# Sliding-window attention feeding a mixture of experts: routing cut into short steps, the first expert slot in plain fp32, and two expert slots in a written-out order

## The chip, the cores and the metric

The kernel runs on one core of a Trainium2 chip. The number that counts is the device time of one execution in microseconds; lower is better. The chip's engines are called by the profile's short names: PE (TensorE, matmuls) with PEld (its weight loads), DVE (VectorE), ACT (ScalarE), POOL (GpSimd) and SP (SyncE, which here only issues transfers).

## The reference

Attention over 4 batches of 8 heads, 768 positions of 64 numbers, with a window of 128 positions and 4 sink positions that are always kept; its output is the input of a mixture of 8 experts, of which each of the 3072 tokens takes one:

```
keep = is_sink | in_window                    # 4 sinks, window 128
a = softmax(where(keep, q @ k.T / 8, -1e9))
x = (a @ v) as 3072 tokens x 512
e_idx = argmax(x @ w_gate)                    # one expert of 8 per token
gate_w = softmax(x @ w_gate)[e_idx]
eom = sigmoid(x @ w_output_gate)[e_idx]
out[token] = gate_w * eom * (relu(x @ w1[e_idx]) @ w2[e_idx])
```

An expert has w1 of 512 x 1024 and w2 of 1024 x 512, 4 MB together, so 8 transfers of 512 KB.

## The kernel before, in words

**Attention.** The 32 (batch, head) pairs are worked as 16 double heads, `NP = 16`. `pair_step(i)` is one step of a software pipeline: in three parts (g = 0, 1, 2) it makes the scores of double head i (PE, mask and maximum on DVE, exponential on ACT), and beside them the transpositions, sink rows, value products, normalisation and gate logits of double heads i-1 and i-2. Steps 16 to 18 have no scores and only drain the pipeline. The sink rows go through `sink`: ACT copies the high part, DVE subtracts the low part, and SP moves both into `psk` by DMA; `av_sink` needs them. In part 1 and 2 POOL scales the next double head's q (`scale`), and at the end of part 2 `gate2` of double head i-2 adds to the logits; with a batch's last double head it calls `batch_done`.

**Routing.** `gate_route` is a generator that works out, for the tokens of batches 0 and 1 together, then of batch 2, then of batch 3, which expert a token takes, its place in the expert's list (matmuls with a triangle of ones), its weight (`den`, written to DRAM beside x), and adds it to a table of token ids (`tab`) by a product of one-hot matrices (`ohrow`, `rhs`). After batch 1 and after batch 2, `rank_experts` orders the experts by their counts and `early_table` takes the rows of the two fullest ones: so expert slots 0 to 3 are fixed before all tokens are known. `final_table` makes the rest of the plan.

**The order of the work.** Everything in attention's loop stands under a manual schedule: PE, ACT, DVE and POOL do it in the order in which the program is written. SP's order, and that of everything behind the loop, is chosen by a scheduler that can also put later instructions between those of the loop. The routing's generators stand in a list `later`; `step()` runs the first one to its next `yield`, once per part g of an attention step (twice per part behind step 15). A list `behind` holds the conversions of weights, one per part.

**Expert slots.** A slot gathers up to 384 tokens by an indirect DMA from POOL (`gather`), turns them (`x_transpose`), and does two products (`mm1_group`, `mm2`). fp32 is split: a number is the sum of a high and a low fp32r part, and a product is three matmuls (high-high, high-low, low-high). So each 512 KB piece of weights goes through a staging buffer (`raw`, four of them), ACT rounds it to the high part and DVE or POOL subtracts to get the low one (`split` in `load_weights`, L454 and L455); the hidden layer is split in the same way (L489, L490), and x too (L484, L485). Slots with 64 tokens or fewer (`half1`, `half2`) use plain fp32 matmuls on the loaded weights (`whole`), with the array's columns in two halves. Weights live in rings of named buffers: a (4), b (3), c (6). Slots 0 and 1 have 256 tokens each.

## Time and profile before

| | us |
|---|---|
| median of 3 runs | 609.74 (605.77 to 613.70) |
| the profiled execution | 610.09 |
| its span | 607.8 |

Busy time in the span: PE 518.4 us (85%), DVE 357.1 (59%), POOL 328.7 (54%), ACT 283.2 (47%). The core moved 112.63 MB by DMA. The profile gives the span in 40 slices with the busy share of each engine in tenths; groups of instructions by line with their count, busy time and mean; the waits that ended last before an instruction (in brackets behind it, with the time its engine stood idle); and the chain of work that ended last. A matmul row's time is its latency; the distance between the starts of two of them is what they cost. Engines other than the one that sets the pace may stand idle at no cost, so shares are read stage by stage.

### The profile page before, as it was taken

How to read it: one execution, taken by the hardware profiler on the slowest of the kernel's cores; microseconds unless marked ns; L12 is line 12 of the kernel's file. 1: busy time of each engine (PE TensorE's matmuls, PEld its weight loads, DVE VectorE, ACT ScalarE, POOL GpSimd, SP SyncE). 2: the span in 40 equal slices, each digit the busy share in tenths (PEclk: the TensorE clock that was granted, in tenths of full speed). 3: DMA queues.
4: the chain of work that ended last, by engine and by line, in shares of the span. 5: the costliest groups of instructions: out<-in, count | busy, mean ns of one | idle time of the engine just before them, and what ended most of it. 6: DMA issues, size and time to landing. Idle time of an engine off the chain costs nothing.

```text
span 607.8 us, 10633 instructions
## 1 busy us (share of the span) xinstructions
PE 518.4 (85%) x3527; PEld 408.4 (67%) x3527; DVE 357.1 (59%) x762; ACT 283.2 (47%) x731; POOL 328.7 (54%) x345
## 2 busy tenths in 40 slices
PE   2999898978887625958899999989998989899992
PEld 1666665655555514947698897779876787777971
DVE  5577677777675589899936255324344736435520
ACT  3576666545444431443555244523352645446410
POOL 6466666746844462275566273573343777557510
PEclk9999999988898565978899999989997999999997
DMA  7378887775739264174685795562396785988660
GB/s 217 98 138 154 191 137 128 181 109 111 135 108 190 38 174 129 36 231 168 206 290 197 237 355 163 188 235 65 119 368 228 244 283 199 343 301 254 214 230 18
DMA packets 68673, 112.63 MB, mean 185 GB/s; under 512 B 8284, under 2 KB 34912, under 8 KB 68610
## 3 DMA queue, kind: packets, MB, share of 16 engines
q1 hardware_dynamic: 64146, 97.94, 56.8%
q0 software_dynamic: 4464, 13.91, 6.5%
q8 instruction: 31, 0.51, 0.4%
q14 instruction: 32, 0.26, 0.1%
HBM read 98.26 MB, written 13.25 MB: 183 GB/s over the span
## 4 chain that ended last, share of the span: by engine, by line
PE 43%; DVE 19%; DMA 15%; issue 9%; POOL 7%; ACT 5%; SPq 1%; POOLq 0%; ACTq 0%; DVEq 0%
PE s L510 16%; DMA raw<-in_w_dram 7%; PE oA L566 6%; PE oB L566 5%; PE s L672 5%; DMA out_dram<-y,idx 3%; PE oA L741 2%; ACT e L684 2%; PE tp L695 2%; DMA psk<-hl 2%; DVE s L678 1%; DVE nmx L682 1%; PE oB L741 1%; DMA xg<-xd,idx_e 1%; DMA xg<-xd,idx 1%
## 5 line engine op out<-in xcount | busy, mean ns | idle before, releaser
L684 ACT ACTIVATE e<-s,nmx 128x132 f32<-128x132 f32 x192 | 69.4, 366 | 76.1 <-DVE nmx L682 57.1
L672 PE MATMUL s<-kr,qr 64*128 64x260 f32 (+1 forms) x384 | 63.2, 438 | 19.1 <-ACT e L684 13.0
L81 POOL TENSOR_SCALAR_AFFINE_SELECT g<-f 128x512 f32<-128x512 f32 (+1 forms) x48 | 27.6, 575 | 72.1 <-ACT f L699 45.4
L490 DVE SCALAR_TENSOR_TENSOR hl<-s,hh 128x512 fp32r<-128x512 f32 (+1 forms) x40 | 29.6, 741 | 60.8 <-ACT hh L489 53.4
L672 PEld LDWEIGHTS s<-kr,qr 64*128 64x128 f32 x384 | 32.6, 203 | 39.8 <-ACT e L684 19.7
L552 POOL DMA_INDIRECT out_dram<-y,idx x20 | 25.2, 1260 | 48.0 <-DMA out_dram<-y,idx 11.7
L489 ACT ACTIVATE hh<-s 128x512 fp32r<-128x512 f32 (+1 forms) x40 | 25.5, 638 | 50.8 <-PE s L510 50.7
L682 DVE TENSOR_REDUCE nmx<-s 128x2 f32<-128x264 f32 x96 | 41.5, 433 | 3.3
L659 POOL TENSOR_SCALAR qr<-qr 128x256 f32<-128x256 f32 x48 | 41.1, 877 | 1.3 <-DMA qr<-in_qT_dram 1.2
L678 DVE COPY_PREDICATED s<-maskf,s 128x256 f32<-128x256 int32 x80 | 33.7, 421 | 11.8 <-PE s L672 8.8
L684 ACT ACTIVATION_READ_ACCUMULATOR e<-s,nmx 128x1 f32 x192 | 37.8, 197 | 0.0
L695 PE MATMUL tp<-ident,e 128*128 128x128 f32 x192 | 31.5, 307 | 5.5 <-ACT f L699 5.5
L695 PEld LDWEIGHTS tp<-ident,e 128*128 128x128 f32 x192 | 23.1, 154 | 17.5 <-ACT f L699 6.4
L81 POOL TENSOR_SCALAR_AFFINE_SELECT f<-f 128x512 f32<-128x512 f32 (+1 forms) x48 | 27.0, 562 | 3.3
L470 POOL DMA_INDIRECT xg<-xd,idx x21 | 24.3, 1158 | 7.2 <-issue 3.5
L741 PE MATMUL oA<-f,vt 128*64 128x128 f32 x256 | 28.0, 299 | 0.0
L455 POOL TENSOR_TENSOR a1l<-raw,a1h 128x1024 fp32r<-128x1024 f32 x5 | 12.3, 2467 | 17.9 <-PE oB L566 16.3
L482 PE MATMUL tp<-ident,xg 128*128 128x128 f32 x100 | 16.7, 298 | 6.1 <-DVE tab L274 3.3
L551 ACT ACTIVATE y<-oA,sc 128x512 f32<-128x512 f32 (+1 forms) x18 | 11.7, 650 | 21.3 <-PE oA L566 14.3
L455 POOL TENSOR_TENSOR a2l<-raw,a2h 128x1024 fp32r<-128x1024 f32 x5 | 14.4, 2880 | 10.1 <-ACT a2h L454 5.8
L741 PE MATMUL oA<-g,vt 128*64 128x128 f32 x192 | 19.5, 283 | 0.0
L741 PEld LDWEIGHTS oA<-f,vt 128*64 128x64 f32 x256 | 15.4, 144 | 6.1 <-issue 4.4
(560 smaller groups left out, 1711.8 us busy)
## 6 DMA issues: line engine op xcount, KB each, us to landing
raw<-in_w_dram SPq DMA_DIRECT2D x104, 512.0 KB
kr<-in_kx_dram SPq DMA_DIRECT2D x16, 396.0 KB
qr<-in_qT_dram SPq DMA_DIRECT2D x16, 384.0 KB
vt<-in_vx_dram SPq DMA_DIRECT2D x16, 384.0 KB
xd<-x SPq DMA_DIRECT2D x16, 384.0 KB
b1h<-in_w_dram SPq DMA_DIRECT2D x2, 512.0 KB
b1l<-in_w_dram SPq DMA_DIRECT2D x2, 512.0 KB
b2h<-in_w_dram SPq DMA_DIRECT2D x2, 512.0 KB
```

Source lines behind the costliest of these rows:

```text
L81: nc.gpsimd.affine_select(out=ap, in_=ap if src is None else src, pattern=pattern, compare_op=op, fill=fill, base=base, channel_multiplier=cm)
L455: b = eng.tensor_tensor(out=lo, in0=raw, in1=hi.bitcast(F32), op=ALU.subtract)
L490: nc.vector.scalar_tensor_tensor(out=lo, in0=ps, scalar=0.0, in1=hi.bitcast(F32), op0=ALU.max, op1=ALU.subtract)
L510: nc.tensor.matmul(out=ps[:, j, 0:n], lhsT=a, rhs=x[:, d, 0:n], start=d == 0 and i == 0, stop=d == ND - 1 and i == 2)
L566: nc.tensor.matmul(out=ys[s], lhsT=h[:, sl], rhs=x, start=f == 0 and i == 0, stop=f == NF - 1 and i == 2)
L659: nc.gpsimd.tensor_scalar(out=q, in0=q, scalar1=SCALE, scalar2=None, op0=ALU.mult)
L672: nc.tensor.matmul(out=s[:, a, o0:P + CW], lhsT=z["q"][r, t * P:(t + 1) * P], rhs=z["k"][r, k0:k0 + P + CW - o0], start=True, stop=True)
L678: nc.vector.copy_predicated(out=both[:, :, 4:CW], mask=bc(maski[:, 1, 4:CW], 1, 2), data=s[:, :, 0:P])
L682: nc.vector.tensor_reduce(out=m, in_=both, axis=AX.X, op=ALU.max, negate=True)
L684: nc.scalar.activation(out=z["e"][:, t, a, :], in_=both[:, a, :], func=AF.Exp, bias=m[:, a:a + 1], scale=1.0, accum_out=z["rs"][:, t, a:a ...
L695: nc.tensor.transpose(out=tp[:, k, :], in_=z["e"][:, 2 * j + k // 2, k % 2, 4:CW], identity=ident)
L741: nc.tensor.matmul(out=o, lhsT=v[:, kt, r], rhs=src[:, kt, a, :], start=t == kt == 0 or t == kt + 1 == 4, stop=False, skip_group_check=True)
```

## The change: what it does

- `gate_route`, `rank_experts`, `early_table` and `final_table` are cut into more and shorter steps, and every `yield` carries a letter. `point(name)` runs the first generator in `later` only if it waits at that letter. The loop has four such places per step: A in `sink` between ACT's high part and DVE's low part; B at the end of part 1; P behind the scores of part 2; C behind `av_sink`, ahead of `gate2`. Behind step 15 two further points per part take any letter.
- Of the three pieces of a one-hot product two go to POOL, issued together at A, and one to DVE at B, for every batch; before, all were POOL's, one per step (for the last batch DVE's).
- The experts are ranked as soon as the counts are known, ahead of the table; `taken` and `base` are updated there. Both expert numbers are read at that time, and 12 transfers of 512 KB are put in `behind`, one per part: slot 0's w1 and w2 straight into the a ring, without staging or split, and slot 1's w1 into the four staging buffers.
- Slot 0 is done in plain fp32 (`plain_x`, `plain1`, `plain2`) on 256 tokens.
- `early_slots` stands under the manual schedule: slots 0 and 1 in a fixed order, with routing steps (four behind each group of slot 0's matmuls, two in slot 1) and the conversions of slot 1's weights between them. The loop has one draining step fewer. `final_table` comes behind these slots; the scheduler may still move it.

```diff
-        def gate_route(bs, lg, e2=nc.vector):
+        def gate_route(bs, lg, counted=None):
...
-            yield
+            yield "A"
...
+            yield "B"
...
+            yield "C"
...
+            tt(out=eq, in0=og, in1=ohb, op=ALU.mult)
+            z = small([P, n], F32, "z")
+            nc.vector.tensor_reduce(out=z, in_=eq, axis=AX.X, op=ALU.add)
+            yield "P"
             nc.scalar.activation(out=dd, in_=dd, func=AF.Exp)
-            yield
+            nc.scalar.activation(out=z, in_=z, func=AF.Exp, scale=-1.0)
...
+            yield "C"
...
+            if counted is not None:
+                counted()
+            yield "A"
+            den = small([P, n], F32, "den")
+            nc.vector.tensor_reduce(out=den, in_=dd, axis=AX.X, op=ALU.add)
...
+                yield "A"
...
-                for t in range(0, T, 2):
-                    e2.tensor_tensor(out=rhs[:, t:t + 2], in0=bc(oh2[:, h + t:h + t + 2].rearrange("p t a e -> p t (a e)"), 3, NJ),
-                                     in1=bc(ohj[:, h + t:h + t + 2], 2, 2 * E), op=ALU.mult)
-                    if t < T - 2:
-                        yield
-                yield
+                for t, eng in ((0, nc.gpsimd), (2, nc.gpsimd), (4, nc.vector)):
+                    if t == 4:
+                        yield "B"
+                    eng.tensor_tensor(out=rhs[:, t:t + 2], in0=bc(oh2[:, h + t:h + t + 2].rearrange("p t a e -> p t (a e)"), 3, NJ),
+                                      in1=bc(ohj[:, h + t:h + t + 2], 2, 2 * E), op=ALU.mult)
+                yield "P"
...
@@ rank_experts, early_table
+            yield "C"
+            if r0:
+                nc.vector.tensor_copy(out=had, in_=taken)
+            for r in range(n):
+                tt(out=taken, in0=taken, in1=perm[:, r0 + r, :], op=ALU.add)
+            nc.vector.scalar_tensor_tensor(out=base, in0=taken, scalar=2.0 * P, in1=base, op0=ALU.mult, op1=ALU.max)
...
-                tt(out=four, in0=four, in1=bc(taken, 1, 4), op=ALU.mult)
+                tt(out=four, in0=four, in1=bc(had, 1, 4), op=ALU.mult)
...
@@ load_weights
+                    if parts:
+                        loads.append(lambda hi=hi, view=view: nc.sync.dma_start(out=hi, in_=view))
+                    else:
+                        nc.sync.dma_start(out=hi, in_=view)
...
+                raws = []
+                def load(view=view, raws=raws):
+                    raws.append(stg.tile([P, kk, n], F32, name="raw"))
+                    nc.sync.dma_start(out=raws[0], in_=view)
+                def cast(pool=pool, name=name):
+                    hi, lo = ((pool or pools[name[0]]).tile([P, kk, n], F32R, name=name + x) for x in "hl")
+                    his.extend(hi[:, j, :] for j in range(kk))
+                    los.extend(lo[:, j, :] for j in range(kk))
+                    return hi, lo
+                def split(raws=raws, cast=cast, eng=nc.vector if i % 2 else nc.gpsimd):
+                    hi, lo = cast()
+                    nc.scalar.copy(out=hi, in_=raws[0])
+                    eng.tensor_tensor(out=lo, in0=raws[0], in1=hi.bitcast(F32), op=ALU.subtract)
                 if parts:
+                    loads.append(load)
                     splits.append(split)
                 else:
+                    load()
                     split()
...
+        def plain1(mp, w, xf, f0):
+            ps = s_tile()
+            for j in range(2):
+                for d in range(ND):
+                    nc.tensor.matmul(out=ps[:, j, 0:2 * P], lhsT=w[0][d][:, (f0 + j) * P:(f0 + j + 1) * P], rhs=xf[:, d, 0:2 * P],
+                                     start=d == 0, stop=d == ND - 1)
+            h = mp.tile([P, 2, HN], F32R, name="hh", bufs=4).bitcast(F32)
+            nc.scalar.activation(out=h[:, :, 0:2 * P], in_=ps[:, :, 0:2 * P], func=AF.Relu)
+            return [h[:, 0], h[:, 1]]
+        def plain2(w, hs, ys, f):
+            for s, y in enumerate(ys):
+                nc.tensor.matmul(out=y, lhsT=hs[f][:, s * P:(s + 1) * P], rhs=w[0][f], start=f == 0, stop=f == NF - 1)
...
@@ ring, loop
+        aa, bb, cc = (["%s%d" % (c, i) for i in range(n)] for c, n in (("a", 4), ("b", 3), ("c", NB)))
+        order = iter(aa + bb + aa + bb[:1] + (cc + bb[1:] + aa + bb[:1]) * NSLOT)
...
                 nc.scalar.copy(out=hl[:, 0, :], in_=tp[0:n, 0, :])
+                point("A")
                 tt(out=hl[:, 1, :], in0=tp[0:n, 0, :], in1=hl[:, 0, :].bitcast(F32), op=ALU.subtract)
...
+            def start_later(g, at):
+                later.insert(at, [g, next(g)])
+            def point(name=None):
+                if later and name in (None, later[0][1]):
+                    x = later[0]
+                    x[1] = next(x[0], None)
+                    if x[1] is None:
+                        later.remove(x)
+                        r = [r for r, (after, n) in enumerate(ROUNDS) if after == b]
+                        start_later(gate_route(bs, bt["lg", bs], lambda: start_later(early_rank(r[0]), 0)) if r
+                                    else gate_route(bs, bt["lg", bs]), len(later))
+                        if r:
+                            start_later(early_rows(r[0]), len(later))
...
+            def early_rank(r):
+                yield from rank_experts(*firsts(r))
                 if r == 0:
-                    ws["e0"] = expert_reg(order_i[0:1, 0:1])
-                    ws[0, 0], rest = load_weights(0, ws["e0"], slot, parts=True)
-                    behind.append(split_later(rest, 4))
-                    yield
-                    yield
+                    for k in range(2):
+                        ws["e%d" % k] = expert_reg(order_i[0:1, k:k + 1])
+                    for j in range(2):
+                        ws[0, j], loads, _ = load_weights(j, ws["e0"], slot, whole=True, parts=True)
+                        behind.extend(loads)
+                    ws[1, 0], loads, splits[1, 0] = load_weights(0, ws["e1"], slot, parts=True)
+                    behind.extend(loads)
+            def early_rows(r):
+                yield from early_table(*firsts(r))
+                if r == 0:
                     ws["xg"] = early_gather(0)
...
+                    if g == 2 and i < NP:
+                        point("P")
...
+                        point("B")
...
+                        if i < NP:
+                            point("C")
                         if have(i - 2):
                             gate2(i - 2)
-                    for _ in range(1 if i < NP else 2):
-                        step()
-                    for x in behind:
-                        next(x, None)
+                    if i >= NP:
+                        if not behind and splits[1, 0][1:]:
+                            splits[1, 0].pop(0)()
+                        for _ in range(2):
+                            point()
+                    if behind:
+                        behind.pop(0)()
+            def early_slots():
...
+                for f in behind:
+                    f()
+                xf = plain_x(mx, ws["xg"])
+                while splits[1, 0][1:]:
+                    splits[1, 0].pop(0)()
+                h0 = []
+                for f0 in range(0, NF, 2):
+                    h0 += plain1(mp, ws[0, 0], xf, f0)
+                    between(4)
+                xg1 = early_gather(1)
+                begin(1, 1)
+                ys = [ps_o.tile([P, DM], F32, name=n) for n in ("oA", "oB")]
+                for f in range(NF):
+                    plain2(ws[0, 1], h0, ys, f)
+                    if f % 2:
+                        between(4, *([splits[1, 0].pop(0)] if f == 1 else [splits[1, 1].pop(0)] if f == 3 else []))
+                for s in range(2):
+                    put(mp, ys[s], ws["xg"][s][1], DM, out, NTOK, ids[0][s][1])
+                xs1 = x_transpose(mx, xg1)
+                h1 = []
+                for f0 in range(0, NF, 2):
+                    h1 += mm1_group(mp, ws[1, 0], xs1, 2, [f0])
+                    between(2, *([splits[1, 1].pop(0)] if f0 in (0, 2, 6) else []))
+                ys = [ps_o.tile([P, DM], F32, name=n) for n in ("oA", "oB")]
+                for f in range(0, NF, 2):
+                    mm2_part(ws[1, 1], h1, ys, (f, f + 1))
+                    between(2)
+                for s in range(2):
+                    put(mp, ys[s], xg1[s][1], DM, out, NTOK, ids[1][s][1])
...
-                for i in range(NP + 3):
-                    pair_step(i)
+                for i in range(NP + 2):
...
-            ws["xs"] = x_transpose(mx, ws["xg"])
-            while later:
-                step()
-            while len(hs0) < NF:
-                more0()
-            for x in behind:
-                for _ in x:
-                    pass
-            ws["e1"] = expert_reg(order_i[0:1, 1:2])
-            ws[1, 0] = load_weights(0, ws["e1"], slot, pin=True)
-            xgs1 = early_gather(1)
-            xs1 = x_transpose(mx, xgs1)
-            early = [[(idx_e[:, 0, r, j:j + 1], idx_e[:, 1, r, j:j + 1]) for j in range(2)] for r in range(NE)]
-            mm2(mp, ws[0, 1], hs0, ws["xg"], early[0])
-            hs1 = mm1(mp, ws[1, 0], xs1, 2)
+                    pair_step(i)
+                early_slots()
...
-            final_table(mp)
-            plan = [(order_i[0:1, r:r + 1], early[r], False) for r in range(NE)]
+            start_later(final_table(mp), len(later))
+            while later:
```

More of the change, by code (lines that the diff above doesn't have):

```diff
@@ L345, in early_table @@
                 nc.vector.tensor_reduce(out=idu[:, r, :], in_=pr, axis=AX.X, op=ALU.add)
-                tt(out=taken, in0=taken, in1=perm[:, r0 + r, :], op=ALU.add)
+            yield "C"
             ide = sm.tile([P, n, 2], F32, name="ide")
@@ L350, in early_table @@
             put_ids(idx_e[:, 0, r0:r0 + n], idx_e[:, 1, r0:r0 + n], ide)
[L351 removed]
         def final_table(mp):
             some = sm.tile([P, E, NJ], F32, name="some", bufs=1)
+            yield "A"
             tt(out=some, in0=bc(base, 2, NJ), in1=iouj, op=ALU.is_gt)
@@ L430, in moe_kernel, with load_weights @@
         w2v = w2.rearrange("e (f p) d -> e p f d", p=P)
-        def load_weights(which, ereg, slot, whole=False, parts=False, pin=False):
-            splits = []
+        def load_weights(which, ereg, slot, whole=False, parts=False):
+            loads, splits = [], []
             src, k, n = ((w1v, ND, FF), (w2v, NF, DM))[which]
@@ L515, in mm1_group, with plain_x, mm2_part @@
             return hs
+        def plain_x(mx, xgs):
+            xf = mx.tile([P, ND, HN], F32R, name="xh", bufs=1).bitcast(F32)
+            for s, (xg, sc) in enumerate(xgs):
+                nc.scalar.copy(out=sc, in_=xg[:, DM:XW])
+                tp = ps_t.tile([P, ND, P], F32, name="tp")
+                for d in range(ND):
+                    nc.tensor.transpose(out=tp[:, d, :], in_=xg[:, d * P:(d + 1) * P], identity=ident)
+                nc.scalar.copy(out=xf[:, :, s * P:(s + 1) * P], in_=tp)
+            return xf
+        def plain1(mp, w, xf, f0):
+            ps = s_tile()
+            for j in range(2):
+                for d in range(ND):
+                    nc.tensor.matmul(out=ps[:, j, 0:2 * P], lhsT=w[0][d][:, (f0 + j) * P:(f0 + j + 1) * P], rhs=xf[:, d, 0:2 * P],
[6 more added lines that the diff above has]
+                nc.tensor.matmul(out=y, lhsT=hs[f][:, s * P:(s + 1) * P], rhs=w[0][f], start=f == 0, stop=f == NF - 1)
+        def mm2_part(w, hs, ys, fs):
+            wh, wl = w
+            for f in fs:
+                hi, lo = hs[f]
+                for s, y in enumerate(ys):
+                    sl = slice(s * P, (s + 1) * P)
+                    for i, (h, x) in enumerate(((hi, wh[f]), (hi, wl[f]), (lo, wh[f]))):
+                        nc.tensor.matmul(out=y, lhsT=h[:, sl], rhs=x, start=f == 0 and i == 0, stop=f == NF - 1 and i == 2)
         def relu_transpose(mp, ps):
@@ L606, in moe_kernel @@
         ws = {}
-        ring = [["%s%d" % (c, i) for i in r] for c, r in (("a", range(2)), ("a", range(2, 4)), ("b", range(3)), ("c", range(NB)))]
-        a0, a1, b0, cc = ring
-        order = iter(a0 + a1 + b0 + a0 + a1 + b0 + a0 + (cc + a1 + b0 + a0) * NSLOT)
+        aa, bb, cc = (["%s%d" % (c, i) for i in range(n)] for c, n in (("a", 4), ("b", 3), ("c", NB)))
+        order = iter(aa + bb + aa + bb[:1] + (cc + bb[1:] + aa + bb[:1]) * NSLOT)
         pools = {"a": wp}
@@ L781, in moe_kernel @@
             later, behind = [], []
-            def split_later(fs, lag):
-                for _ in range(lag):
-                    yield
-                for f in fs:
-                    f()
-                    yield
-            def step():
-                if later and next(later[0], later) is later:
-                    later.pop(0)
+            def start_later(g, at):
[6 more added lines that the diff above has]
+                        later.remove(x)
             def batch_done(b):
@@ new lines, in pair_step, with between, begin @@
+                    if behind:
+                        behind.pop(0)()
+            def early_slots():
+                ids = [[(idx_e[:, 0, r, j:j + 1], idx_e[:, 1, r, j:j + 1]) for j in range(2)] for r in range(NE)]
+                ws["ids"] = ids
+                def between(n, *fs):
+                    for f in fs:
+                        f()
+                    for _ in range(n):
+                        point()
+                def begin(k, j):
+                    ws[k, j], loads, splits[k, j] = load_weights(j, ws["e%d" % k], slot, parts=True)
+                    for f in loads:
+                        f()
+                for f in behind:
+                    f()
+                xf = plain_x(mx, ws["xg"])
[25 more added lines that the diff above has]
+                    put(mp, ys[s], xg1[s][1], DM, out, NTOK, ids[1][s][1])
@@ L1074, in moe_kernel @@
             steps = []
-            for k in range(1, n):
-                if k > 1 and k not in ahead:
+            for k in range(2, n):
+                if k not in ahead:
                     steps.append((first, k))
```

67 lines of the change are left out of this document (24 added, 43 removed).

## The prediction

> **What bounds the kernel now.** I read the page's slices first, then a table of stages, then VectorE's timeline inside the attention loop, then the chain of waits for the prices.
>
> ```profile
> span 607.8 us, 10633 instructions
> PE   2999898978887625958899999989998989899992
> DVE  5577677777675589899936255324344736435520
> ```
>
> One slice is 15.2 us. Counted from 0, TensorE is nearly full up to slice 11, thin in 12 to 17 (7, 6, 2, 5, 9, 5), and full again from slice 20. VectorE has its 8s and 9s just there, in slices 14 to 19. The stage table (length, then busy time of PE, PEld, DVE, ACT, POOL, then clock, DMA share, GB/s) puts sizes on it:
>
> ```profile
> 72.00:104.00 32.00, 29.91 (x291) 20.10 (x291) 22.86 (x59) 20.02 (x88) 19.89 (x36) 1.00 0.79 145
> 114.75:200.50 85.75, 67.70 (x603) 46.33 (x599) 58.33 (x165) 42.22 (x185) 48.55 (x82) 0.91 0.64 130
> 200.50:238.70 38.20, 17.53 (x114) 12.24 (x114) 31.90 (x96) 12.03 (x22) 20.62 (x19) 0.59 0.48 113
> 238.70:304.90 66.20, 54.79 (x310) 48.18 (x311) 63.01 (x178) 27.49 (x38) 32.15 (x15) 0.87 0.50 165
> 304.90:600.00 295.10, 279.14 (x1612) 235.20 (x1610) 126.27 (x112) 132.19 (x193) 156.21 (x85) 0.98 0.66 232
> ```
>
> The rows are: the undisturbed attention loop; attention steps 10 to 15, where routing is mixed in (L, below); draining attention until the first expert matmul (D); expert slots 0 and 1 (S); the other slots. The first and the last are TensorE's. D and S are VectorE's: 31.90 of 38.20 us and 63.01 of 66.20. All that the change edits lies in L, D and S, 190 us together.
>
> Now L. These are VectorE's rows from step 9 into step 11; an L676 row opens a step.
>
> ```profile
> 104.09 0.49 DVE L676 COPY_PREDICATED_SCALAR s<-maskf,none 128x264 f32 x1 [0.15 <-PE s L672]
> 107.68 0.28 DVE L723 TENSOR_TENSOR hl<-oA,hl 40x128 fp32r<-40x128 f32 x1 [0.96 <-ACT hl L722]
> 111.24 0.43 DVE L678 COPY_PREDICATED s<-maskf,s 128x256 f32<-128x256 int32 x1 [0.61 <-PE s L672]
> 114.23 0.36 DVE L182 TENSOR_TENSOR lw<-tp,rs 128x192 f32<-128x192 f32 x1 [1.29 <-PE tp L180]
> 114.75 0.50 DVE L676 COPY_PREDICATED_SCALAR s<-maskf,none 128x264 f32 x1 [0.15 <-PE s L672]
> ...
> 118.55 0.23 DVE L208 TENSOR_REDUCE m<-lg 128x12 f32<-128x96 f32 x1
> 120.69 0.25 DVE L218 TENSOR_TENSOR dd<-lg,m 128x96 f32<-128x96 f32 x1
> ...
> 123.53 0.19 DVE L228 TENSOR_REDUCE den<-dd 128x12 f32<-128x96 f32 x1
> 124.37 0.17 DVE L236 TENSOR_TENSOR base<-tp,base 128x8 f32<-128x8 f32 x1
> ...
> 129.19 0.28 DVE L238 TENSOR_TENSOR pos<-pos,ohb 128x96 f32<-128x96 f32 x1
> 130.33 0.23 DVE L243 RECIPROCAL den<-den 128x12 f32<-128x12 f32 x1 [0.21 <-DVE den L242]
> 130.48 0.46 DVE L676 COPY_PREDICATED_SCALAR s<-maskf,none 128x264 f32 x1
> ```
>
> Step 9 takes 114.75 - 104.09 = 10.66 us and holds three idle times of VectorE: 0.96, 0.61 and 1.29. Step 10 takes 15.73, 5.07 more. Its routing comes in three lumps, 118.55 to 120.94, 123.53 to 124.54 and 129.19 to 130.56: 2.39 + 1.01 + 1.37 = 4.77. So nearly all of a lump is paid in full: it stands ahead of the next score's mask, and TensorE waits for that.
>
> **L, the loop.** The new points are just those idles: A in front of the 0.96, B at the 0.61, C in front of the 1.29, P without VectorE work. At 10.66 a step, steps 10 to 15 would take 64.0. To that I add what does not fit:
> - The first lump's six pieces take 0.40 each, the second's five 0.20. In step 10 A has two (0.8 of 0.96), B two (0.2 over the 0.61), C two of either kind (1.2 of 1.29). Ranking, positions and weights are cut in like pieces: I allow 0.4 over in each of steps 11 to 13, and 0.8 once for the position matmuls and two exponentials now at P. Sum 2.2.
> - Steps 14 and 15 hold the one-hot products, priced by these rows:
>
> ```profile
> L265 POOL TENSOR_TENSOR rhs<-oh,ohj 128x512 bf16<-128x512 bf16 x9 | 11.0, 1226 | 2.0 <-DVE oh L258 2.0
> L265 DVE TENSOR_TENSOR rhs<-oh,ohj 128x512 bf16<-128x512 bf16 x3 | 6.4, 2152 | 0.0
> 139.22 0.90 DVE L262 TENSOR_TENSOR ohrow<-io,jf 128x768 bf16<-128x768 f32 x1
> 215.52 3.09 DVE L262 TENSOR_TENSOR ohrow<-io,jf 128x768 bf16<-128x768 f32 x1
> ```
>
> The third product goes to VectorE at B: 2.15 - 0.61 = 1.5 over; for the table's six matmuls at P I allow 0.5. Two steps: 4.0. The 0.90 for ohrow just fits A; if GpSimd blocks it as in the 3.09 row, 2.2 more per step. GpSimd's two products, 2.45 us, delay the scaling of q; I count 0.5. [...]
> - DMA. Twelve loads of 512 KB (first slot whole, half of the second) are now issued one per third of a step from step 12, 6.3 MB in some 50 us, 126 GB/s. Free room behind the last q and k loads:
>
> ```profile
> 160.00:180.00 20.00, 17.35 (x156) 11.69 (x151) 13.67 (x40) 9.06 (x40) 13.74 (x22) 0.91 0.26 72
> 65.65 4.63 DMA psk<-hl
> ```
>
> Share 0.26 after step 13; before it 0.79 with 145 GB/s, which leaves less than the loads ask for one step. SyncE's queue is passed by them, and the sink rows' transfer (psk, 4.63 us) sits behind them. Between 0 and one landing per step (4.09, below), that is 0 to 16; I take 2, since only step 13 is oversubscribed.
>
> L after: 64.0 + 2.2 + 4.0 + 0.5 + 2 = 73, from 85.75: **13 saved** (0 to 20).
>
> **D, the drain.** One thing here leaves for certain: ScalarE's copy for the first slot's gather stood in front of attention's exponentials.
>
> ```profile
> 198.70 0.19 ACT L479 COPY sc<-xg 128x1 f32<-128x1 f32 x1 [4.07 <-DMA xg<-xd,idx_e]
> 200.93 1.33 PE L695 MATMUL tp<-ident,e 128*128 128x128 f32 x5 [5.50 <-ACT f L699]
> 224.01 0.15 DVE L298 SCALAR_TENSOR_TENSOR u<-taken,base 128x8 f32<-128x8 f32 x1
> 228.76 0.16 DVE L351 SCALAR_TENSOR_TENSOR base<-taken,base 128x8 f32<-128x8 f32 x1
> 230.82 0.19 DVE L208 TENSOR_REDUCE m<-lg 128x6 f32<-128x48 f32 x1
> 234.28 0.13 DVE L249 CAST pi<-tokpos 128x6 int32<-128x6 f32 x1
> ```
>
> (That 5.5 lies at the end of L; the copy is now behind the drain. It makes L's number safer, and I don't count it twice.) In D itself the order is now fixed: two short passes of attention, up to 15 points, and three of the second slot's conversions. VectorE's work there: the first rows of the table about 2.6; batch 2's routing to its positions 3.5 (230.82 to 234.28) and about 1.2 behind; ranking 2.0 (part of the 4.9 from 224.01); attention's own pieces about 5 (by the rows of step 9); one conversion 1.2 to 3.2: some 16 us. Beside it runs attention's own chain through psk's 4.63; two passes without scores should not be longer than two steps of L, 21. I take 19 for D (14 to 26), against 38.20: **19 saved**. The conversions of slot 0 and the routing of batch 3, which filled D, are gone or behind.
>
> **S, the two slots.** Prices of TensorE, from the chain of waits:
>
> ```profile
> 238.69 7.40 PE s L510 x46
> 250.04 2.82 PE s L510 x24
> 303.64 0.70 PE oA L566 x3
> 469.11 3.58 PE s L585 x16
> 377.45 4.09 DMA raw<-in_w_dram
> L485 DVE TENSOR_TENSOR xl<-tp,xh 128x512 fp32r<-128x512 f32 x25 | 16.5, 681 | 4.8 <-ACT xh L484 4.8
> L490 DVE SCALAR_TENSOR_TENSOR hl<-s,hh 128x512 fp32r<-128x512 f32 (+1 forms) x40 | 29.6, 741 | 60.8 <-ACT hh L489 53.4 <-issue 7.2
> L455 DVE TENSOR_TENSOR a1l<-raw,a1h 128x1024 fp32r<-128x1024 f32 x4 | 12.6, 3161 | 4.0 <-issue 4.0
> ```
>
> A slot in three split products costs 4 x 2.82 + 16 x 0.70 = 22.5; two make 45.0, so S loses 21 us to VectorE today. Plain fp32: L585 does eight half-width matmuls of 512 columns (16 records) in 3.58, two halves of the array side by side if they overlap. A full one then takes 3.58 / 4 = 0.90, or 0.45 if they don't. Slot 0 has 16 + 16 of that size: 28.6, or 14.3. I take 28.6, as the rows nearest in kind share the array by halves. So fp32 costs 6.1 more on TensorE. It takes off VectorE four conversions (up to 3.16 each), two 0.68 and four 0.74: 9 to 17 us, in the engine that bounds S. S after: 28.6 + 22.5 + a cold start 2.0 (46 matmuls in 7.40, at 2.82 / 24 they are 5.4) + 3 for turning the second slot's rows between the slots (four dependent pieces like the 0.68) + 4 for waits at the 20 routing steps left = **60, 6 saved** (-8 to 20). The final table's work on VectorE moves behind S; slots 2 and 3 hide it, whose rows don't need it (without that cover it would lengthen the stage by its own time, as in S before).
>
> The other slots keep their code. Four staging buffers serve slot 1 until its first product is over, so slot 2's last load may come late: 0 to 4.09 + 3.16; I take 2.
>
> **Sum:** 13 + 19 + 6 - 2 = 36 off the profiled run's 610.09 us (span 607.8): 574. The runs' median, 609.74, is 0.35 less: **574 us**, 5.9% less. A measurement of this kernel can tell about 2% from no change, so below 597.5 is faster and above 622 slower.
>
> **Rivals.** (1) The loop keeps its length: the loads collide with psk, or GpSimd blocks VectorE's steps (3.09 against 0.90). For it: share 0.79. Against it: share 0.26 from step 13. L's 13 are lost: 587. (2) The fixed order makes TensorE wait at the routing steps between the matmuls, as S lost 21 us before; S is then 28.6 + 22.5 + 21 + 5 = 77, so 17 worse: 591. Against it: plain fp32 needs no VectorE between its matmuls. (3) Slower: those same waits keep the clock at half. It was 0.59 in D, and the cold start shows its price. If the 51 us of matmuls in S run at half, they take 51 more: 625. It decides from 36 us at half on. Against it: the 24 matmuls at 250.04 already ran at the speed of later slots. [...] (4) Both (1) and (2): 604, no measurable change. (5) The change does better: the split halves of L585 don't overlap, 14.3 off: 560.
>
> **Chances:** forecast 0.57 (own range 562 to 583), (1) 0.13, (2) 0.12, (3) 0.03, (4) 0.08, (5) 0.07. Faster 0.89, same 0.08, slower 0.03. Range 550 to 594: it holds the forecast, (1), (2) and (5), and goes below (5) for L's and D's upper bounds together.
>
> **What will show it.** L: steps 10 to 13 at 10.7 to 11.5 us, 14 and 15 below 13.5; no VectorE routing row over 1 us at A or C; psk not among TensorE's waits. D: the first expert matmul 17 to 22 us behind the last exponential, no ACT wait for xg among exponentials. S: plain fp32 matmuls of 512 columns 0.90 us apart and VectorE well under 63 busy us. It is wrong if steps 10 to 15 stay over 80 us, if S stays over 66, or if slot 2 starts more than 5 us behind slot 1's end.

## The result, and the profile after

586.5 us (median of four runs, 583.9 to 588.8) against 609.4 us before (four runs). The ratio is 0.962, with an interval of 0.954 to 0.970. The profiled run took 584.36 us, its span was 582.1 us, 25.7 less than the 607.8 before. So the kernel is faster, and the time lies in the range, but some 12 us above the forecast of 574. The stages show that the total hides two misses and a gain that nobody forecast.

The first view is the table by stage of the kernel after: attention steps 10 to 15 (L), the drain up to the first expert product (D), slots 0 and 1 (S), and the other slots up to the last scaled output. The columns are the stretch, its length, the busy time of PE, PEld, DVE, ACT and POOL, the granted clock, the DMA share and GB/s.

```profile
114.16:198.28 84.12, 62.83 (x591) 42.65 (x589) 56.36 (x154) 41.50 (x182) 45.03 (x77) 0.88 0.77 172
198.28:219.42 21.14, 12.22 (x114) 8.28 (x110) 16.37 (x61) 8.22 (x18) 11.84 (x14) 0.79 0.63 133
219.42:287.94 68.52, 59.26 (x276) 44.01 (x276) 59.83 (x215) 22.67 (x36) 29.83 (x20) 0.94 0.39 122
287.94:571.90 283.96, 273.73 (x1613) 231.03 (x1611) 115.91 (x112) 133.24 (x194) 154.68 (x85) 1.00 0.69 242
```

Of the kernel before, the other slots up to the same end, and its first two rows of expert products:

```profile
304.87:597.61 292.74, 279.17 (x1612) 235.22 (x1610) 126.30 (x112) 132.19 (x193) 155.23 (x84) 0.98 0.67 233
235.29 0.80 PE L510 MATMUL s<-xh,a0h 128*128 128x256 f32 x2 [0.76 <-ACT xh L484]
238.69 0.58 PE L510 MATMUL s<-xl,a0h 128*128 128x256 f32 x1 [2.61 <-DVE xl L485]
```

Against the rows of before: L is 1.6 us shorter (forecast 13), D 17.1 (19), S 2.3 longer (forecast 6 shorter). The other slots, from 304.87 to 597.61 us before, were 292.7 us and are 284.0, 8.7 less (forecast 2 more). With the 0.6 that step 10 starts earlier these are the 25.7. One boundary matters: the prediction's D ends at 238.7 us, but the kernel before made a first pair of expert products at 235.29 and then waited 2.61 us. Measured to the first product, as after, D is 13.7 us shorter and S 1.1 shorter; their sum is the same.

L is not slow everywhere. By the first masks of the steps, steps 10 to 15 last 10.3, 10.7, 11.1, 29.6, 12.2 and some 10 us. What is lost lies in step 13. The next rows are of that step: TensorE's wait, VectorE's end of the sink rows, and SyncE's issues (start, time).

```profile
173.65 0.66 PE L815 MATMUL oA<-psk,vst 64*128 64x384 f32 x1 [17.68 <-DMA psk<-hl]
150.12 0.28 DVE L790 TENSOR_TENSOR hl<-oA,hl 40x128 fp32r<-40x128 f32 x1
145.52 0.37 SPq L469 DMA_DIRECT2D a0h<-in_w_dram  x1
...
153.62 0.37 SPq L469 DMA_DIRECT2D a3l<-in_w_dram  x1
154.61 0.47 SPq L479 DMA_DIRECT2D raw<-in_w_dram  x1
155.95 3.43 SPq L250 DMA_DIRECT2D xd<-den  x2
159.49 4.15 SPq L792 DMA_DIRECT2D psk<-hl  x3
```

The sink rows were ready at 150.4. SyncE issued them from 159.5, behind nine weight loads (eight tiles of slot 0 and one of slot 1, 4.7 MB, all between 145.5 and 155.1) and behind two writes of the gates' factors (den). They landed only some ten us after that. The written order puts one load behind each third of a step, but that order binds TensorE, ScalarE, VectorE and GpSimd, not SyncE: in the program's data the loads depended on nothing but the expert's number, and the scheduler put them together. The stretch in slices of 5 us shows two kinds of full DMA engines:

```profile
150.00:155.00 5.00, 5.00 (x56) 3.74 (x54) 4.58 (x15) 2.02 (x10) 4.27 (x6) 1.00 1.05 375
155.00:160.00 5.00, 0.97 (x18) 0.73 (x14) 1.20 (x5) 1.91 (x9) 0.81 (x2) 0.96 1.04 395
165.00:170.00 5.00, 0.00 (x0) 0.00 (x0) 0.00 (x0) 0.00 (x0) 0.00 (x0) 0.50 1.18 84
```

First weights at 375 to 395 GB/s, later a share of 1.18 at 84 GB/s. In S the rows to read are plain fp32's pace and the one long wait inside slot 0:

```profile
254.06 1.02 PE L573 MATMUL oB<-a3l,hh 128*128 128x512 f32 x2
254.91 0.59 PE L573 MATMUL oA<-a3l,hh 128*128 128x512 f32 x1
239.52 3.37 DVE L490 TENSOR_TENSOR a0l<-raw,a0h 128x1024 fp32r<-128x1024 f32 x1
242.82 0.95 DVE L268 TENSOR_TENSOR ohrow<-io,jf 128x768 bf16<-128x768 f32 x1
243.82 0.28 PE L278 MATMUL tp<-rhs,ohrow 128*128 128x256 bf16 x1 [3.52 <-DVE ohrow L268]
246.00:248.00 2.00, 2.00 (x4) 0.88 (x3) 2.00 (x13) 0.12 (x1) 0.00 (x0) 0.50 0.62 251
273.83 0.39 PE L542 MATMUL s<-xh,b0h 128*128 128x256 f32 x1 [2.91 <-DVE hl L522]
```

Two records make one product of 512 columns, 0.85 us apart (0.86 over several). One conversion of slot 1's weights stands ahead of the one-hot rows on VectorE, and TensorE waits 3.5 us for them; the clock is at half behind that.

### The profile page after: what moved, and what is told of

Same layout as the page of the kernel before. It is cut to its first block, busy times and chain, and to the rows that moved or that the text cites. A ratio compares the mean times of both kernels' runs of the same rounds, so it can differ in the third digit from the quotient of the medians.

```text
span 582.1 us, 10501 instructions
## 1 busy us (share of the span) xinstructions
PE 507.0 (87%) x3479; PEld 392.2 (67%) x3479; DVE 326.1 (56%) x754; ACT 274.8 (47%) x723; POOL 313.5 (54%) x340
## 5 line engine op out<-in xcount | busy, mean ns | idle before, releaser
L738 PE MATMUL s<-kr,qr 64*128 64x260 f32 (+1 forms) x384 | 61.9, 430 | 13.2 <-ACT e L750 6.6
L522 DVE SCALAR_TENSOR_TENSOR hl<-s,hh 128x512 fp32r<-128x512 f32 (+1 forms) x36 | 26.7, 747 | 58.7 <-ACT hh L521 49.6
L738 PEld LDWEIGHTS s<-kr,qr 64*128 64x128 f32 x384 | 31.9, 201 | 34.6 <-ACT e L750 15.6
L619 POOL DMA_INDIRECT out_dram<-y,idx x20 | 23.4, 1170 | 48.4 <-DMA out_dram<-y,idx 8.5
L521 ACT ACTIVATE hh<-s 128x512 fp32r<-128x512 f32 (+1 forms) x36 | 22.9, 642 | 30.4 <-PE s L542 30.4
L761 PE MATMUL tp<-ident,e 128*128 128x128 f32 x192 | 30.2, 296 | 0.0
L761 PEld LDWEIGHTS tp<-ident,e 128*128 128x128 f32 x192 | 22.2, 149 | 10.7 <-issue 5.4
L808 PE MATMUL oA<-f,vt 128*64 128x128 f32 x256 | 26.4, 285 | 0.0
L182 DVE TENSOR_TENSOR lw<-tp,rs 128x192 f32<-128x192 f32 x16 | 5.7, 354 | 34.3 <-PE tp L180 34.3
L815 PE MATMUL oA<-psk,vst 64*128 64x384 f32 x16 | 7.2, 450 | 19.3 <-DMA psk<-hl 19.2
L618 ACT ACTIVATE y<-oA,sc 128x512 f32<-128x512 f32 (+1 forms) x18 | 11.7, 650 | 22.1 <-PE oA L633 14.3
L818 ACT COPY ot<-oA 128x512 f32<-128x512 f32 x16 | 9.6, 599 | 22.8 <-PE oA L815 19.3
L765 ACT COPY f<-tp 128x512 f32<-128x512 f32 x32 | 18.6, 582 | 0.7 <-PE tp L761 0.7
```

Of the source, the lines that this page charges most:

```text
L521: nc.scalar.activation(out=hi, in_=ps, func=AF.Relu)
L522: nc.vector.scalar_tensor_tensor(out=lo, in0=ps, scalar=0.0, in1=hi.bitcast(F32), op0=ALU.max, op1=ALU.subtract)
L619: nc.gpsimd.indirect_dma_start(out=where, out_offset=bass.IndirectOffsetOnAxis(ap=ids, axis=0), in_=y, in_offset=None, bounds_check=rows - ...
L738: nc.tensor.matmul(out=s[:, a, o0:P + CW], lhsT=z["q"][r, t * P:(t + 1) * P], rhs=z["k"][r, k0:k0 + P + CW - o0], start=True, stop=True)
L761: nc.tensor.transpose(out=tp[:, k, :], in_=z["e"][:, 2 * j + k // 2, k % 2, 4:CW], identity=ident)
L808: nc.tensor.matmul(out=o, lhsT=v[:, kt, r], rhs=src[:, kt, a, :], start=t == kt == 0 or t == kt + 1 == 4, stop=False, skip_group_check=True)
```

## Experiments

Twelve kernels. Step lengths and stretches are of their profiled runs. L runs from step 10's first mask to the last exponential, D from there to the first expert product, S from there to slot 2's first product; "rest" from there to the last scaled output.

**1. Paced loads.** GpSimd touches each weight tile ahead of its load, so that the written order binds the load too.

```
+    nc.gpsimd.memset(hi[:, 0, 0:1], 0.0)
     nc.sync.dma_start(out=hi, in_=view)
...
+    nc.gpsimd.memset(raws[0][:, 0, 0:1], 0.0)
     nc.sync.dma_start(out=raws[0], in_=view)
```

> Edit: a one-element write by GpSimd into each of the twelve weight tiles goes ahead of its load, so that the load cannot start before GpSimd's written order reaches that third of a step. Theory (nine of the twelve loads left SyncE in one burst at the start of step 13, and step 13's three psk copies stood behind them): psk's wait falls from 17.7 us to 2 us or less, step 13 lasts 11 to 13 us instead of 29.6, steps 10 to 15 last 66 to 70 us in all, and the time is 567 to 573 us. Rival (6.3 MB of weights do not fit beside the loop's own transfers at any pace): psk's wait is spread over steps 13 to 15, steps 10 to 15 last 78 us or more, and the time is 579 to 586 us.

Measured: 580.8 us, ratio 0.959 (0.953 to 0.965). L is 70.7 us instead of 84.0, step 13 is 15.8, and its wait is 4.1. SyncE's issues of step 13 and the wait (paced kernel):

```profile
148.92 0.35 SPq L471 DMA_DIRECT2D a0h<-in_w_dram  x1
150.20 0.77 SPq L797 DMA_DIRECT2D psk<-hl  x1
151.08 1.00 SPq L250 DMA_DIRECT2D xd<-den  x2
152.13 1.67 SPq L797 DMA_DIRECT2D psk<-hl  x2
160.36 0.41 PE L820 MATMUL oA<-psk,vst 64*128 64x384 f32 x1 [4.12 <-DMA psk<-hl]
113.79:184.58 70.79, 61.52 (x591) 42.02 (x589) 56.32 (x154) 41.62 (x182) 45.32 (x86) 0.98 0.88 168
```

So the burst cost L 13 us, and for the loop the theory holds but for the last 2 us of wait. For the whole it failed: the profiled span is only 4.2 us shorter, and the ratio is not clear of the changed kernel's 0.962. D took back 2.8 (24.0), S 1.4 (69.95), the rest 3.1, and the last output's end 2.2. What remains of psk's wait is not the burst.

**2. All loads behind the loop** (on experiment 1).

```
+    for _ in range(4 if i >= NP else 0):
         if behind:
             behind.pop(0)()
```

> Edit: as the paced one, and all twelve loads come after the last score, four behind each third of the first drain step. Theory of the burst: steps 10 to 15 last 64 to 67 us, no psk wait above 1 us; 6.3 MB at the 375 to 395 GB/s of the burst take 16 to 17 us and end inside the drain's 20 us, so the time is 565 to 570 us. Rival (the loads then stand in front of the last rows' writes and the first gather): the drain grows from 19.9 us to 25 us or more, and the time is 572 to 580 us.

Measured: 594.9 us, ratio 0.979 (0.974 to 0.984). The rival, and worse than it said: the first load left at 197.9 us, 9.3 behind the last exponential, and D was 36.5 us. The surprise is in the loop. With no weight moving, step 13 was 17.6 us:

```profile
155.00:160.00 5.00, 3.44 (x42) 2.46 (x38) 3.33 (x13) 2.58 (x13) 2.29 (x5) 1.00 0.85 78
160.00:165.00 5.00, 0.88 (x3) 0.58 (x4) 0.00 (x0) 0.19 (x1) 0.32 (x1) 0.70 1.00 100
164.12 0.66 PE L820 MATMUL oA<-psk,vst 64*128 64x384 f32 x1 [5.68 <-DMA psk<-hl]
```

The DMA engines are nearly full (share 0.85 and 1.00) at 78 to 100 GB/s. What had been issued there beyond every step's own transfers were den's two writes, 768 packets of 4 bytes each. That these packets made the wait is an estimate from these rows; how they would fill the engines the rows do not show. Experiments 5, 6 and 9 move them.

**3. Routing's points at the ends of the thirds** (on experiment 1).

```
-    point("A") ... point("P") ... point("B") ... point("C")
+    else:
+        for _ in range(2 if g == 2 else 1):
+            point()
```

> Edit: as the paced one, and the same short steps of routing are taken at the ends of a step's three thirds (one, one and two), as the kernel before took its long ones, instead of at the four points inside. Theory of the prediction (each piece is paid where it stands ahead of the next score's mask): steps 10 to 15 are 10 to 18 us longer than in the paced kernel, some 80 us, and the time is 579 to 588 us. Rival (short pieces and the three products on GpSimd are what helps, the place is not): steps 10 to 15 within 4 us of the paced kernel's, and the time within 5 us of it.

Measured: four runs from 590.7 to 603.5 us. The profiled run took 601.4 us; its L is 84.6 us, 13.9 above experiment 1. The clock was full until 114 us and 0.75 to 0.91 in several stretches behind that; whether that came of the waits in the loop or of the run is not known, so the 13.9 are no price. The shortest run points the same way: 590.7 is 5.7 above the slowest and 11.1 above the fastest of experiment 1 (579.6 to 585.0). It is a single run, so the places' worth is shown in its direction, not in its size.

**4. Routing ahead of the conversion in slot 0** (on experiment 1).

```
-    between(4, *([splits[1, 0].pop(0)] if f == 1 else ...))
+    if f == 1:
+        between(4)
+    between(0 if f == 1 else 4, *([splits[1, 0].pop(0)] if f == 1 else ...))
```

> Edit: as the paced one, and in slot 0's second product the four steps of routing come ahead of the 3.4 us conversion of slot 1's weights on VectorE instead of behind it. Theory (that conversion holds the one-hot rows back, TensorE waits 3.5 us for them and then runs at half clock for some 5 us): the wait falls below 1.5 us, slots 0 and 1 last 3 to 6 us less than in the paced kernel, and so does the whole. Rival (TensorE waits for something else next: the table's pieces, or the converted weights at slot 1's start): the stretch stays within 1.5 us of the paced kernel's.

Measured: 584.0 us, ratio 0.961 (0.954 to 0.969). The 3.5 us wait went, and slot 0 ended 4.9 us sooner behind its first product (31.5 against 36.4 to the first scaled output). A new wait stood at slot 1's rows, and S came to 71.0 us:

```profile
246.40 1.04 ACT L494 CAST c1h<-raw 128x1024 fp32r<-128x1024 f32 x1 [3.76 <-DMA raw<-in_w_dram]
248.79 0.47 PE L519 MATMUL tp<-ident,xg 128*128 128x128 f32 x1 [6.80 <-DVE xl L522]
```

The rival. c1h is a tile of slot 2: its conversion is bound by no written order, the scheduler put it among slot 1's work, and ScalarE stood before it until its load had landed.

**5. The factors behind psk.** The short steps with den and with the position bits change places, on the paced kernel.

```
     yield "A"
+    pi ... ji
+    yield "B"
     den ... (two writes)
-    yield "B"
-    pi ... ji
```

> Edit: as the paced kernel, and two short steps of the routing are exchanged, so that batch 0 and 1's factors (den, two writes of 768 packets of 4 bytes) are computed and written at point B, behind all three psk copies, instead of at point A, between the first copy and the other two. Theory (what is left of the wait in step 13 is those packets: in the kernel with all weights behind the loop psk still waited 5.7 us, with 78 to 100 GB/s at a share of 0.85 to 1.00): psk's wait falls from 4.1 us to 1 us or less, step 13 from 15.4 us to 11 to 12.5, steps 10 to 15 from 70.7 us to 66 to 68, the whole is 3 to 4 us shorter than the paced kernel. Rival (the weights of that step make the wait, or the packets now stand before the next step's tiles): a wait of 3 us or more in step 13 or 14, the time within 1.5 us of the paced kernel's.

Measured: 581.5 us, ratio 0.960 (0.956 to 0.964), no change against the paced kernel. No long psk wait was left in step 13 (11.1 us), and 3.7 us of wait stood in step 14 (16.0): L 71.1. The rival's second form: the wait came a step later, with the DMA engines at shares of 1.36 and 1.20 and 150 and 98 GB/s from 170 to 174 us.

**6. The same exchange without pacing**, in the changed kernel.

```
     yield "A"
+    pi ... ji
+    yield "B"
     den ... (two writes)
```

> Edit: the exchange of those two short steps alone, in the changed kernel, whose weights leave in a burst. Theory (both causes, the burst the larger: 4.7 MB ahead of psk at 375 to 395 GB/s are 12 us): psk's wait falls from 17.7 us to 9 to 13, step 13 from 29.6 us to 21 to 25, steps 10 to 15 from 84 us to 76 to 80, the time 579 to 583 us. Rival (the small packets are nearly all of it, and with them behind psk the burst is covered): psk's wait 5 us or less, steps 10 to 15 72 us or less, and the time within 2 us of the paced kernel with the exchange.

Measured: 586.7 us, ratio 0.967 (0.962 to 0.971). psk's wait was 11.3 us instead of 17.7, step 13 was 23.2, L 81.2, as the theory of two causes has it for the step (L is 1.2 over its bound). The time is no shorter than the changed kernel's, which neither said; the profiled run's S was 69.7 and its rest 285.3, each a little longer.

**7. The final table in the written order** (on experiment 5).

```
+    if f == 0:
+        while later: point()
+        start_later(final_table(mp), 0)
+    between(3)
```

> Edit: as the paced kernel with the exchange, and the pieces of the final table, which no order binds and which the scheduler puts between slot 0's and 1's, are written into the order behind slot 1's first group of the second product. Theory (the table's some 150 pieces make VectorE the late engine in slots 0 and 1, 59.9 us busy of 68.5): TensorE's waits of 3.5 us for the one-hot rows and 3.0 us for hl shrink to under 1.5 us each, slots 0 and 1 last 3 to 6 us less than with the exchange alone, and half of that or more is left in the whole. Rival (ScalarE's conversions of slot 2's weights, which wait 5.9 and 3.8 us for their loads ahead of other work, hold slot 1 as well, or slot 4's indices come late): the stretch is at most 1.5 us shorter, or the later slots give it back, and the time is within 2 us.

Measured: 584.8 us, ratio 0.968 (0.964 to 0.973). S fell to 60.6 us, what the prediction had said of it, and the wait for the one-hot rows to 2.5. But slots 2 and 3, 23.7 and 21.9 us apart in experiment 5, took 29.4 and 27.4, and the rest was 298.0 us instead of 288.5; in slot 2 TensorE now waited 3.2 and 3.6 us. Its S against the stretch behind it:

```profile
208.68:269.27 60.59, 56.62 (x275) 43.19 (x276) 29.53 (x59) 22.34 (x36) 26.51 (x19) 0.96 0.48 137
269.27:330.00 60.73, 51.48 (x317) 45.59 (x316) 55.17 (x168) 21.79 (x33) 26.55 (x16) 0.94 0.62 204
```

VectorE's load moved by one stage, and its price with it.

**8. One conversion behind the turning of rows** (on experiment 5).

```
-    if not behind and splits[1, 0][1:]:
+    if not behind and splits[1, 0][2:]:
```

> Edit: as the paced kernel with the exchange, and the third conversion of slot 1's weights (b2h, before which ScalarE waited 8.7 us for a load in the paced kernel) comes behind the turning of slot 0's rows instead of ahead of it. Theory: from the last exponential to the first expert product 21 us or less instead of 24, and the whole 2 to 3 us shorter than with the exchange alone. Rival (slot 0's own weights and rows come no earlier): the stretch stays at 23.5 us or more, or slots 0 and 1 give it back; the time within 1.5 us.

Measured: 575.6 us, ratio 0.951 (0.947 to 0.956), the fastest whose results are whole; beside the changed kernel's 0.962 the intervals still touch. D is 22.0 us instead of 24.5, where 21 or less was expected. The rows are ScalarE's, in the paced kernel and then here:

```profile
205.02 1.04 ACT L494 CAST b2h<-raw 128x1024 fp32r<-128x1024 f32 x1 [8.71 <-DMA raw<-in_w_dram]
205.97 0.19 ACT L558 COPY sc<-xg 128x1 f32<-128x1 f32 x1
```

```profile
203.89 0.58 ACT L562 COPY xh<-tp 128x512 f32<-128x512 f32 x1 [1.04 <-PE tp L561]
204.37 1.05 ACT L494 CAST b2h<-raw 128x1024 fp32r<-128x1024 f32 x1
```

The median gains 5.9 us on experiment 5 where 2 to 3 were expected. D explains 2.5; in the profiles 2.3 more lie in L, whose code is the same, so that part is not shown to be the edit's.

**9. No factors in the loop** (on experiment 8).

```
-    for j, b in enumerate(bs):
+    for j, b in enumerate(bs if len(bs) == 1 else ()):
```

> Edit: as the kernel with the late conversion, but the factors of batches 0 and 1 are not written in the loop; ones are written in their place in step 3, so that the results of these batches are left unscaled and the work is otherwise the same. The time of the whole is not to be read, only steps 10 to 15. Theory (the 1536 packets of 4 bytes are all that is left of psk's wait, which followed them from step 13 to step 14): no psk wait above 1 us from step 10 on, step 14 from 14.6 us to 11.5 or less, steps 10 to 15 from 68.8 us to 65 to 66.5. Rival (two and three weights to a step are enough to hold psk): step 14 stays above 13.5 us with a psk wait of 2 us or more.

Measured: steps 13 and 14 last 11.1 and 12.5 us, and neither shows a psk wait; L is 67.3 us. This is the theory, but for 1.0 of step 14, 0.8 of L and a wait of 1.5 us in step 11, before any weight: den's packets are what is left of psk's wait in steps 13 and 14, and two or three paced weights to a step are hidden. The two writes went to step 3 here, and the wait went with them: at 53.06 us TensorE waited 4.0 us for psk, with no weight on its way, and step 10 starts 4.8 us later than in experiment 8.

**10. ScalarE issues psk** (changed kernel, not paced).

```
-    nc.sync.dma_start(out=psks[p % 2]...
+    nc.scalar.dma_start(out=psks[p % 2]...
```

> Edit: in the changed kernel, nothing paced, the three psk copies are issued by ScalarE instead of SyncE. Theory of the queue (psk was late because it stood behind nine weights in SyncE's order, issued at 159.5 us where its data were there at 150.1): psk's wait falls from 17.7 us to 3 or less, steps 10 to 15 from 84 us to 74 or less, and the time is 573 to 579 us. Rival (the sixteen DMA engines are what is full; whoever issues, psk's packets stand behind the weights' in them): psk's wait 8 us or more, the time 582 to 588 us.

Measured: 599.2 us, ratio 0.988 (0.982 to 0.995), worse than either said. Every step costs a us more (steps 7 to 9 at 11.5 instead of 10.3 to 10.7), as ScalarE now spends some 2 us on issuing (three issues of 0.68 us), and step 10 starts 8.1 us later; these are most of the 12.6 us that the profiled run lost. L is 85.3 us, 1.3 more than the changed kernel's, and step 13 is 27.0: the burst still held it. In step 13 ScalarE stood still itself:

```profile
161.34 0.27 ACT L788 CAST hl<-oA 40x128 fp32r<-40x128 f32 x1
167.22 6.20 ACTq L792 DMA_DIRECT2D psk<-hl  x3
173.46 0.37 ACT L174 COPY lgT<-oB 96x256 f32<-96x256 f32 x1 [11.85 <-DMA psk<-hl]
```

psk's data was ready at 161.6, and the first issue came at 167.2. What held the issues back in between was not shown. In the changed kernel's burst SyncE, by its profile, waited ahead of den's two writes 0.8 us each for the landings of a0l and a1h.

So the first theory is out: with psk on another queue its first issue still came 5.6 us behind its data, and ScalarE stood 11.85 us for it. SyncE's order is not the whole of the delay. A wait of 8 us or more is what the second theory expected, but the time is some 11 us above its 588, and no run takes apart full DMA engines and what the issues themselves waited for.

**11. The conversion of experiment 4 on GpSimd** (on experiment 8).

```
-    between(4, *([splits[1, 0].pop(0)] if f == 1 ...
+    between(4, *([lambda g=splits[1, 0].pop(0): g(eng=nc.gpsimd)] if f == 1 ...
```

> Edit: as the kernel with the late conversion, and the last conversion of slot 1's first weights (a0l, 3.4 us on VectorE ahead of the one-hot rows) is made by GpSimd. Theory: TensorE's wait of 3.5 us for the one-hot rows falls below 1.5 us, the half clock behind it goes, slots 0 and 1 last 66 to 67.5 us instead of 69.7, and the ratio to the kernel before is 0.945 to 0.948 instead of 0.951. Rival (GpSimd makes two of the three products of the one-hot rows, and its conversion now stands ahead of them, 2.4 us long; or the gain waits again at slot 1's rows): the stretch stays within 1 us, and so does the time.

Measured: 580.5 us, ratio 0.957 (0.952 to 0.962). The wait for the one-hot rows fell to 1.6 us, the clock stayed full behind it, and S was 74.7 us, 5.0 longer than in experiment 8. The wait is again at slot 1's rows, behind the same unbound conversion, and behind it the matmuls of 256 columns stood 0.21 us apart up to 255.3 us, and 0.12 from 255.6 on:

```profile
244.29 1.04 ACT L494 CAST c1h<-raw 128x1024 fp32r<-128x1024 f32 x1 [5.84 <-DMA raw<-in_w_dram]
246.54 0.58 PE L547 MATMUL s<-xh,b0h 128*128 128x256 f32 x1 [8.40 <-ACT xh L521]
```

**12. Slot 2's first conversions in the written order** (on experiment 11).

```
+    if f0 == 2:
+        begin(2, 0)
+    if f0 >= 4:
+        splits[2, 0].pop(0)()
...
+    between(2, *([splits[2, 0].pop(0)] if f < 4 else []))
```

> Edit: as the kernel with GpSimd's conversion, and the loads and conversions of slot 2's first weights (c0h to c3h) are written into the order inside slot 1 (behind its third and fourth group and its first two pairs of the second product), where before no order bound them and ScalarE stood 13.4, 5.8, 3.0 and 3.3 us before them for loads, ahead of slot 1's rows and hl. Theory (these unbound conversions are what the waits moved to): TensorE's wait of 8.4 us at slot 1's rows falls below 2, slots 0 and 1 last 62 to 66 us, and the ratio to the kernel before is 0.935 to 0.945. Rival (slot 2's weights are then late, since the buffers they are loaded into come free one by one): the gain is given back by a wait of 4 us or more at slot 2's first product, and the ratio is 0.950 to 0.960.

Measured: 583.8 us, ratio 0.960 (0.956 to 0.965). S fell to 64.9 us and the 8.4 us wait was gone. Slots 2 and 3 then took 27.4 and 25.6 us (22.1 and 23.1 in experiment 11), and the rest was 298.7 us. The rival in its sum, not in its form: no single wait of 4 us, but 13.9 us over the later slots.

## Why the prediction was right, and where not

**L.** The term that failed is DMA's: of 0 to 16, "I take 2, since only step 13 is oversubscribed". The pace of "one per third of a step" was taken from the written order, which does not hold SyncE, as the description of the kernel itself says. Measured, this term is 13.3 us for the burst (experiment 1), and 1 to 4 more for den's packets, which the sum did not have (L is 67.3 without them in experiment 9, and 68.5 to 71.2 in the paced loops with them). The free room, share 0.26 "after step 13", was read from 160 to 180 us, but that lies in steps 13 and 14 (156.5 to 184.2 us by their first masks); step 15 had 0.87. What happened in L is the first rival, by its first mechanism, and L over 80 us was one of the prediction's own signs of being wrong. The other terms were right, on the safe side: with the loads paced L is 70.7 where 73 was forecast. Steps 10 to 12 came at 10.3 to 11.1 us as said, and the one short run of experiment 3 supports the price of a piece in front of a mask. "psk not among TensorE's waits" was the sign to look at, and it was the one that was broken.

**D.** 21.2 us, forecast 19 (14 to 26). Nothing speaks against the reasons: VectorE's work in it came at 16.4 us, where some 16 were forecast and 31.9 stood before, and the last exponentials no longer wait for the gather. But no run takes them apart, and by the first product as it stood before, the gain is 13.7 us and not 17.1. In the kernels with paced loads it was 20.3 to 24.5, by what ScalarE converted ahead of the gathered rows.

**S.** 68.5 us, forecast 60 (its saving was bounded by -8 to 20). Plain fp32 was right: 32 products at 0.86 are 27.5, forecast 28.6, and the fifth rival's 0.45 is out. From the rows, slot 0's 37.2 us are 27.5, some 2.6 of a cold start (forecast 2.0), 3.5 of wait, 1.7 lost in 3.4 us at half clock behind it, and 1.7 of the routing's own products; turning the rows took 4.3 (forecast 3); slot 1 took 26.9 where 22.5 was its product, with waits of 2.9 and 0.85. So the step that failed is "4 for waits at the 20 routing steps left": with the half clock and the routing's products it was some 11. This is the second rival's mechanism at about half its price, and S over 66 us was another sign of being wrong. "Plain fp32 needs no VectorE between its matmuls" is true, but the routing's own products stand between them on TensorE and do. And "The final table's work on VectorE moves behind S" was wrong: its pieces begin at 233.8 us, inside slot 0, since no order binds them, and VectorE is busy 59.8 us of 68.5 (forecast: well under 63). Experiment 7 made that sentence true, and S came to 60.6.

**Other slots.** Forecast 2 us lost, measured 8.7 gained. The rest was 283 to 289 us in every experiment but 3, 7 and 12. One stretch stands out: from 449.9 to 482.6 us the kernel before, with a 3.0 us wait at 458.86 and half clock behind it, took 32.7 us; the changed kernel and all experiments but 3 and 12 took 27.8 to 29.4. Over this whole stage the kernel before ran 10.2 us at half clock (3.4 from 399.53, 6.8 from 457.56 us), the changed kernel none; that is worth 5.1 us at most, an estimate from the granted clock. Why those waits are gone was not tried.

**The whole.** 1.6 + 17.1 - 2.3 + 8.7 + 0.6 = 25.7, against 36. That the time lies in the range is in part luck: with the 2 us lost in the other slots that were forecast, instead of 8.7 gained, the same L, D and S give 597 us, outside it. The three edits do what they say; what was not followed is the work that the edits leave unbound.

## What to carry to other kernels

An order that is written out binds only the engines and the instructions that are in it: before counting on a pace, ask which queue issues the transfer and what the transfer waits for, and give it a dependence if it has none. A stage that is put in order still shares its engines with whatever the scheduler hoists from the stages behind it, and experiments 4, 7, 11 and 12 only moved such a wait into the next slot: follow a removed wait one stage further before counting it. Count packets as well as bytes: in experiment 2 psk waited 5.7 us in the step in which 6 KB went out in 4-byte pieces and no weight moved, and in experiment 9, with the paced weights but without these pieces, no psk wait stood in steps 13 and 14.

## What was not expected of the hardware

The granted clock behind a wait of TensorE did not go by the wait's length alone. In experiments 11 and 12 the same matmul waited the same 1.64 us; the clock then stayed full in the one and fell to half in the other (first two stretches of 2 us behind it in experiment 11, then the wait and a stretch behind it in experiment 12):

```profile
226.00:228.00 2.00, 1.63 (x7) 0.97 (x7) 2.00 (x3) 0.00 (x0) 2.00 (x2) 1.00 0.67 254
228.00:230.00 2.00, 2.00 (x6) 0.95 (x5) 1.90 (x13) 0.00 (x0) 0.63 (x1) 1.00 0.00 0
```

```profile
227.98 0.38 PE L278 MATMUL tp<-rhs,ohrow 128*128 128x256 bf16 x2 [1.64 <-DVE who L393]
230.00:232.00 2.00, 2.00 (x4) 0.97 (x3) 1.90 (x7) 0.00 (x0) 1.24 (x1) 0.50 0.01 3
```

Behind a wait of 3.44 us at that matmul (experiment 6) products of 512 columns stood 0.86 us apart, as at full clock, and behind 3.52 us (after) the clock was 0.50. Elsewhere eight transpositions behind a wait of 1.50 us (experiment 5, at 135.73 us) took 1.97 us, against 1.09 a step earlier; behind 2.91 (after, at 273.83) and 2.99 us (experiment 9, at 261.29) the clock was 1.00.

The lengths of the stretches at half clock repeat. The kernel after has three of them, without the one at its end: 20.48 us from 159.55, 13.65 from 210.75 and 3.41 from 244.88. The kernel before has eleven: six of 3.41 us, two of 6.83, and one each of 10.24, 13.65 and 17.07. The wait of 3.52 us is followed by one of 3.41 us, which at half clock is a loss of 1.7, an estimate. What sets these lengths, and which wait is followed by such a stretch, was not shown: the waits of 1.50 to 3.52 us above came with and without one.

The third rival counted from 36 us at half clock in S on. The kernel after had 8.4 us of it there, 4.99 from 219.42 and 3.41 from 244.88, at a mean clock of 0.94.
